# An attention block with a computed bias and two MLPs: key and value loads placed between the first bias rows, three bias rows of VectorE placed one softmax later

## The chip, the cores and the metric

The kernel runs on one core of a Trainium2 chip. The metric is the device time of one execution in microseconds (us); several runs give a median, and one further execution was recorded by the hardware profiler.

## What is computed

The reference, cut to what matters here (B, H, S, D = 2, 8, 576, 64):

```python
scores = scale * np.matmul(q, k.transpose(0, 1, 3, 2))
pos = np.arange(S)
rel = (pos[:, None] - pos[None, :]).astype(np.float32)
psi_rel = np.log1p(np.abs(rel))
psi_i = np.log1p(np.maximum(pos[:, None].astype(np.float32), 1.0))
x = (psi_rel / psi_i)[..., None]
h = np.maximum(x @ w1 + b1, 0.0)          # hidden 32
bias = h @ w2                             # one value per head
scores = scores + bias.transpose(2, 0, 1)[None, :, :, :]
attn = softmax(scores)                    # written out with max, exp, sum
out = np.matmul(attn, v)
x = out.transpose(0, 2, 1, 3).reshape(B * S, H * D)
x = gated MLP of RMS-normalized x         # 512 -> 1536 -> 512, weights in float64
return squared-ReLU MLP of x              # 512 -> 2048 -> 512, weights in float64
```

The bias depends on the head and on the two positions alone, so it is computed once for both batches.

## The kernel before, in words

**Bias rows.** The 576 query positions are cut into 36 groups g of 16. For each group `hidden(g)` makes four tiles `hq` (128 partitions: 4 positions by 32 hidden units), each one multiply and max over the key distances (L182 on VectorE, on ScalarE by L178 for some of the early groups, and the fourth tile on GpSimd from group 12 on). `bias_mm(g)` (L202) multiplies them with w2 on TensorE, and `bias_out(g)` (L221 on ScalarE; L219 on VectorE for group 20 alone) takes the result to a tile `br` with one row for each position and head. The first eight groups go straight to their place: the DMA at L229 writes `br` into every eighth partition of the bias tile (`bias[0][g:P:8]`, 16 partitions of 8 heads). Later groups go to DRAM (`rows<-br`, L225) and come back shifted into place (`bias<-rows`, L239), again into every eighth partition.

**Attention.** A unit u is a tile of 128 queries (nine tiles, four head pairs each: 36 units). `scores_mm(u)` (L261) writes two PSUM tiles from a ring of two, so it waits until the softmax of the unit before has read them. `soft(u, e)` on VectorE (L273) adds the bias and takes the maximum, `expo` on ScalarE (L280) takes the exponential, the transposes (L289, L291, L316) turn the result, copies (L298, L318) bring it to SBUF, and `values_mm(u)` (L339) multiplies with the values. Units 0 to 7 use the bias tile of the first 128 positions (groups 0 to 7), units 8 to 15 that of groups 8 to 15, and so on. So `soft(0, 0)` needs all eight direct bias rows, and `soft(8, 0)` needs the rows of groups 8 to 15, which went over DRAM.

**Order.** The order on every engine is written out by hand. A first loop over s from -2 to 7 does one unit in a step; step s holds the bias of one group (`groups(s)`: at s = -2 groups 0 to 7, at s = -1 groups 8 to 10, then group s + 11), the scores and softmax of unit s + 1, the transposes of unit s, the hidden tiles of group s + 13 and the values of unit s - 1. A second loop from s = 8 (`PAIRED`) on does two units in a step. At its start `finish` steps (L359 to L390) also normalize the attention output of a finished tile and turn it for the MLP: `finish_c` (L386 transposes on TensorE) needs `finish_n` (L380 on VectorE).

**Loads.** All transfers named here are issued by SyncE (the queue SP), in order. Keys and values are loaded head pair by head pair and batch (`load_k(n)`, 288 KB, and `load_v(n)`, 320 KB, n from 0 to 7; units 0 to 7 use n = u, and later units use the same tiles again). `load_k(0)`, `load_k(1)` and `load_v(0)` stand at the start; the others stand at the head of the steps, as the diff shows.

Of the kernel before, what the change touches and what calls it, by code (L numbers as in the profile page):

```python
# [45 lines left out]
PAIRED = 8  # L46
# [6 lines left out]
def tile_kernel(ctx: ExitStack, tc: tile.TileContext, q, k, v, ltab, lg, cst, cst2, rms_g, wg, wv, wo, win, wo2, s_p, b_p, out):  # L53
    nc = tc.nc
# [51 lines left out]
    cb = ac.tile([P, 2], F32, name="cb")  # L106
    spot = ac.tile([P, 1], F32, name="spot")
    owed = []
    g_row = tab_p.tile([1, DM + P], F32, name="g_row")
    mh = const.tile([P, 1], F32, name="mh")  # L110
    g_bc = const.tile([P, DM], F32, name="g_bc")
# [23 lines left out]
    def load_k(n):  # L135
        ks[n] = ac.tile([P, S], F32, name=f"ks{n}")
        nc.sync.dma_start(out=ks[n], in_=k[:, n])

    def load_v(n):
        t = ac.tile([P, 10, D], F32, name=f"vs{n}")  # L140
        nc.sync.dma_start(out=t, in_=v[:, n])
        vs[n] = t
# [23 lines left out]
    def reach(g):  # L166
        return S if g < 8 else max(16 * g + 15, S - 1 - 16 * g) + 1

    def hidden(g, owed):
        hms[g] = []  # L170
        d = reach(g)
        for tq in range(4):
            n = 4 * g + tq
            hq = h_p.tile([P, S], F32, name="hq")[:, :d]
            src = near[:, P - 1 - 4 * n:P - 1 - 4 * n + S] if g < 8 else tab[:, :d]
            hms[g].append(hq)
            if tq == ACT_QUAD and g in ACT_EARLY:
                nc.scalar.activation(hq, src, AF.Relu, bias=nthr[:, n:n + 1], scale=w1_sb)  # L178
                continue

            def go(eng, hq=hq, src=src, n=n):
                eng.tensor_scalar(hq, src, w1_sb, thr[:, n:n + 1], op0=ALU.mult, op1=ALU.max)  # L182

            if tq != POOL_QUAD or g < POOL_FROM:
                go(nc.vector)
            elif owed is None:
                go(nc.gpsimd)
            else:
                owed.append(lambda go=go: go(nc.gpsimd))
# [58 lines left out]
    def chunk(u):  # L248
        tt = TILES[u // 4]
        return tt // 2 if tt < 8 else 4  # L250
# [14 lines left out]
    def soft(u, e, ps):  # L265
        if u % 4 == 0 and e == 0:
            sums[u // 4] = st_p.tile([P, H], F32, name="rs")
        if e == 0:
            prs[u] = pr_p.tile([P, 2 * S], F32, name="pr")
        h = 2 * (u % 4) + e  # L270
        sn = sn_p.tile([P, S], F32, name="sn")
        nm = st_p.tile([P, 1], F32, name="nm")
        nc.vector.tensor_tensor_reduce(out=sn, in0=ps, in1=bias[chunk(u)][:, h, :],  # L273
                                       scale=-1.0 / SCALE, scalar=3.0e38, op0=ALU.add, op1=ALU.min, accum_out=nm)
        sns[u, e] = sn, nm
# [179 lines left out]
    for g in range(AHD, NG):  # L455
        plan[g - 11 if g > 10 else -1].append(g)

    def hide(g, owed=None):
        if g < NG:
            hidden(g, owed)  # L460

    def s_view(i):
        return reg[:, :16 * TJ].rearrange("p (s i c t) -> p s i c t", s=4, i=2, c=2)[:, :, i]
# [34 lines left out]
    for g in range(LEAD):  # L498
        hide(g)
        if g == 0:  # L500
            nc.scalar.activation(cb[:, 0:1], pcb[:, 0:1], AF.Copy, scale=SCALE)
            nc.scalar.activation(cb[:, 1:2], pcb[:, 0:1], AF.Copy, scale=m_sb)
    def groups(s):
        for g in plan[s]:
            pb = bias_mm(g)
            bias_out(g, pb)
            if s == -1 and g == AHD:
                hide(11)
            if s == -2:
                hide(g + LEAD)  # L510

    for s in range(-2, PAIRED):
        r = s % 4
        if s >= 5 and r == 1:
            finish_a(s // 4 - 1)
        if s >= 0 and r == 0:
            load_q(s // 4 + 1)
        if -1 <= s < 5:
            load_k(s + 3)
        if 0 <= s < 7:  # L520
            load_v(s + 1)
        landed = list(rows)[:2 if s > 3 else 1]
        if s != -1:
            groups(s)
        for g in landed:
            bias_in(g)
        if s >= 6 and r == 2:
            finish_b(s // 4 - 1)
        if 0 <= s + 1 < NU:
            ps = scores_mm(s + 1)  # L530
            if s == -1:
                groups(s)
                nc.tensor.matmul(pg, g_row[:, DM:], g_row[:, :DM], start=True, stop=True)
            soft(s + 1, 0, ps[0])
        if 0 <= s < NU:
            turn_out(s, 0, turn_mm(s, 0))
        if s == 7:
            finish_n(0)
        if 0 <= s + 1 < NU:
            expo(s + 1, 0)  # L540
            soft(s + 1, 1, ps[1])
        if 0 <= s < NU:
            for e in (1, 2):
                turn_out(s, e, turn_mm(s, e))
        if 0 <= s + 1 < NU:
            expo(s + 1, 1)
        if s == 0:
            nc.scalar.copy(g_bc, pg)
        if s >= 6 and r == 2:
            finish_s(s // 4 - 1)  # L550
        if s >= -1:
            hide(s + 13)
        if s == 4:
            nc.sync.dma_start(out=s_sb, in_=s_p)
            nc.sync.dma_start(out=b_sb, in_=b_p)
        if 0 <= s - 1 < NU:
            values_mm(s - 1)
        if s >= 5 and r == 1:
            finish_t(s // 4 - 1)
        if s == 6:  # L560
            xs = [act_p.tile([P, NKC, NT], F32R, name=f"xs{i}", tag=f"x{i}") for i in range(2)]
        if s >= 7 and r == 3:
            finish_c(s // 4 - 1)
# [7 lines left out]
    def wait_for(t):  # L571
        nc.gpsimd.tensor_copy(out=spot, in_=t)

    for s in range(PAIRED, NU + 2, 2):
        tile_ends = s % 4 == 0 and s <= NU - 4
        hiding = s + 13 < NG
        if s % 4 == 0:
            load_q(s // 4 + 1)
        for g in list(rows):
            bias_in(g)  # L580
        if s + 1 < NU:
            ps = scores_mm(s + 1)
            for e in range(2):
                soft(s + 1, e, ps[e])
            if s % 4 == 2:
                finish_s(s // 4 - 1)
        for d in range(2):
            if s - 2 + d > PAIRED - 2:
                values_mm(s - 2 + d)
            if s + 1 < NU:  # L590
                expo(s + 1, d)
            if d and tile_ends:
                finish_a(s // 4 - 1)
            if d:
                hide(s + 13, owed)
                hide(s + 14, owed)
            groups(s + d)
        if s in BITS:
            part = bits_of(BITS[s])
        next(part, None)  # L600
        if s % 4 == 0 and (s, 0) in SUMS:
            wait_for(bits_out())
            s_do(*SUMS[s, 0])
        if s % 4 == 2 and not hiding and s < 34:
            finish_n(s // 4 - 1)
            if (s, 0) in SUMS:
                wait_for(fin[s // 4 - 1][0][:, :1])
                s_do(*SUMS[s, 0])
        if s % 4 == 2 and hiding:
            finish_n(s // 4 - 1)  # L610
        if s + 2 < NU:
            ps = scores_mm(s + 2)
            for e in range(2):
                soft(s + 2, e, ps[e])
                if e == 0 and owed:
                    wait_for(sns[s + 2, 0][1])
                    while owed:
                        owed.pop(0)()
        mid = {}
        if s + 2 < NU:  # L620
            mid = {"e0": lambda: expo(s + 2, 0), "e1": lambda: expo(s + 2, 1)}
        if tile_ends:
            mid["fin"] = lambda: finish_t(s // 4 - 1)
        if s % 4 == 2 and s < 34:
            mid["fin"] = lambda: finish_c(s // 4 - 1)
        if s == 36:
            finish_c(7)
        if s % 8 == 4:
            for g in list(rows)[:1]:
                bias_in(g)  # L630
        turns(s, mid)
        if tile_ends:
            finish_b(s // 4 - 1)
            if (s, 1) in SUMS:
                wait_for(ris[0][:, :1])
                s_do(*SUMS[s, 1])
        if s % 4 == 2:
            next(part, None)
        if s == 34:
            finish_n(s // 4 - 1)  # L640
        if s == 26:
            gen.close()
            wpools["ab"] = ring(ctx, "wab", 2)
            wpools["sp"] = ring(ctx, "wsp", 4)
            u_p = pool(ctx, "u", 1)
            reg_p = pool(ctx, "reg", 1)
            reg = reg_p.tile([P, 6 * NT], F32R, name="reg", tag="reg")
            us = [u_p.tile([P, 2, TJ], F32, name=f"us{i}", tag=f"u{i}") for i in range(4)]
        for at, fn, n in TAIL:
            if at == s:  # L650
                fn(n)
        if s == 34:
            s_do(*SUMS[s, 1])
        if s == 34:
            sco.close()
            psC = ring(ctx, "psC", 4, space=PSUM)
# [455 lines left out]
```

## Time and profile before

| | before |
|---|---|
| median of 3 runs | 596.91 us (596.03 to 598.53) |
| the profiled execution | 597.67 us, span 595.7 us |
| TensorE busy | 587.0 us, 99% |
| VectorE busy | 441.7 us, 74% |
| ScalarE busy | 337.8 us, 57% |
| GpSimd busy | 239.1 us, 40% |

The span is the time from the first to the last instruction in the profile; the profiled execution's own time lies 2.0 us above it. PE is TensorE's matmuls, PEld its weight loads, DVE is VectorE, ACT ScalarE, POOL GpSimd, SP SyncE. Busy is the share of time in which an instruction runs; a busy engine need not be the one that others wait for. In a row of the trace, what stands in brackets at the end is the engine's idle time before the instruction and what ended it.

### The profile page before, as it was taken

To read this page: it belongs to the slowest core of one execution; us is meant where nothing else is said; L and a number is where in the kernel's file an instruction comes from. 1 tells how busy PE (TensorE), PEld (TensorE's weight loads), DVE (VectorE), ACT (ScalarE), POOL (GpSimd) and SP (SyncE) were. 2 spreads that over 40 slices of the span, in tenths; PEclk is the share of its full clock that TensorE was granted. 3 is DMA by queue.
4 is the path that set the end of the run, shared out by engine and by line. 5 is a ranking of instruction groups with operands and counts; after the bars stand their busy time and mean duration, and the time that the engine had idled before them with its cause. 6 is when DMAs were issued, how large, how long until landed. Compare 5 with 4: busy or idle time off the path is not lost.

```text
span 595.7 us, 13412 instructions
## 1 busy us (share of the span) xinstructions
PE 587.0 (99%) x5366; PEld 529.9 (89%) x5366; DVE 441.7 (74%) x789; ACT 337.8 (57%) x678; POOL 239.1 (40%) x222
## 2 busy tenths in 40 slices
PE   9999899999999999999999999999999999999997
PEld 5466666667789999999999999999999999999996
DVE  7977989977776887788787944559995336999541
ACT  8887688887775555555656432246662235665110
POOL 0522255450566655655644432323333233333320
PEclk9999999999999999999999999999999999999999
DMA  7898446475012232233223222212222322222321
GB/s 207 260 301 247 154 141 180 142 233 136 24 53 72 72 111 102 72 104 109 72 73 106 84 95 106 89 54 95 83 72 106 107 72 70 72 100 78 127 87 53
DMA packets 25743, 67.26 MB, mean 113 GB/s; under 512 B 3121, under 2 KB 4689, under 8 KB 25682
## 3 DMA queue, kind: packets, MB, share of 16 engines
q1 hardware_dynamic: 25634, 66.40, 34.7%
q8 instruction: 42, 0.69, 0.5%
q14 instruction: 19, 0.16, 0.1%
q10 hardware_dynamic: 48, 0.02, 0.0%
HBM read 53.21 MB, written 10.83 MB: 108 GB/s over the span
## 4 chain that ended last, share of the span: by engine, by line
PE 86%; DMA 5%; DVE 3%; ACT 3%; POOL 1%; issue 1%; SPq 0%; DVEq 0%; ACTq 0%; POOLq 0%
PE c L736 11%; PE c L712 8%; PE c L713 8%; PE c L711 8%; PE b L736 7%; PE po L339 6%; PE b L712 6%; PE b L713 6%; PE b L711 6%; PE a L261 5%; PE b L289 4%; DMA vs<-in_v 3%; PE b L202 3%; PE po L712 2%; PE po L713 2%; PE po L711 2%
## 5 line engine op out<-in xcount | busy, mean ns | idle before, releaser
L447 POOL TENSOR_TENSOR wlo<-wa,whi 128x512 fp32r<-128x512 f32 (+1 forms) x71 | 95.7, 1351 | 75.1 <-ACT whi L444 75.1
L421 POOL TENSOR_SCALAR wa<-wa 128x512 f32<-128x512 f32 x68 | 47.6, 700 | 125.4 <-ACT wa L420 123.1
L273 DVE CUSTOM_DVE_ANT_0 sn<-a,bias 128x576 f32<-128x576 f32 x72 | 51.6, 753 | 16.5 <-PE a L261 8.2
L280 ACT ACTIVATE pr<-sn,nm 128x576 f32<-128x576 f32 x72 | 56.6, 788 | 12.4 <-DVE nm L273 12.4
L420 ACT ACTIVATE wa<-wraw 128x512 f32<-128x512 f32 x68 | 45.9, 676 | 31.1 <-DMA wraw<-in_wo 28.0
L444 ACT CAST whi<-wa 128x512 fp32r<-128x512 f32 x68 | 42.0, 617 | 23.1 <-DVE wa L432 22.9
L182 POOL TENSOR_SCALAR hq<-tab,c_sb,thr 128x384 f32<-128x384 f32 (+17 forms) x24 | 43.5, 1819 | 28.7 <-PE b L202 28.7
L429 DVE TENSOR_SCALAR wa<-wa 128x512 int32<-128x512 int32 x46 | 28.8, 625 | 31.5 <-POOL wa L421 31.5
L712 PE MATMUL c<-f,whi 128*128 128x384 f32 (+1 forms) x150 | 49.7, 331 | 0.0
L713 PE MATMUL c<-f,wlo 128*128 128x384 f32 (+1 forms) x150 | 49.7, 331 | 0.0
L711 PE MATMUL c<-f,whi 128*128 128x384 f32 (+1 forms) x150 | 49.7, 331 | 0.0
L736 PE MATMUL c<-xs,whi 128*128 128x384 f32 x184 | 46.8, 335 | 0.0
L261 PE MATMUL a<-ks,q 64*64 64x352 f32 (+1 forms) x576 | 44.6, 415 | 0.2 <-ACT br L221 0.2
L969 DVE SCALAR_TENSOR_TENSOR f<-hv,b_sb,f 128x384 fp32r<-128x384 f32 x48 | 40.8, 854 | 1.9 <-ACT f L968 1.8
L339 PE MATMUL po<-pt,vs 128*32 128x128 f32 (+1 forms) x1344 | 41.0, 264 | 0.0
L339 PEld LDWEIGHTS po<-pt,vs 128*32 128x32 f32 x1344 | 33.2, 110 | 8.8 <-issue 8.3
L965 DVE SCALAR_TENSOR_TENSOR hv<-sg,s_sb 128x384 f32<-128x384 f32 x48 | 36.4, 758 | 5.9 <-ACT sg L964 5.9
L289 PE MATMUL b<-ident,pr 128*128 128x128 f32 x288 | 39.3, 279 | 1.1 <-DVE br L219 1.1
L261 PEld LDWEIGHTS a<-ks,q 64*64 64x64 f32 x576 | 19.3, 132 | 23.1 <-issue 5.3
L792 POOL TENSOR_TENSOR tl<-ut,th 128x512 fp32r<-128x512 f32 x20 | 25.9, 1296 | 33.4 <-ACT th L791 21.8
L289 PEld LDWEIGHTS b<-ident,pr 128*128 128x128 f32 x288 | 30.8, 141 | 9.3 <-issue 7.7
L736 PE MATMUL b<-xs,whi 128*128 128x384 f32 x152 | 38.7, 335 | 0.0
(201 smaller groups left out, 1649.4 us busy)
## 6 DMA issues: line engine op xcount, KB each, us to landing
wraw<-in_wo SPq DMA_DIRECT2D x28, 512.0 KB, 3.5
bias<-rows SPq DMA_DIRECT2D x32, 288.0 KB, 4.6
rows<-br SPq DMA_DIRECT2D x28, 295.5 KB, 3.1
wraw<-in_win SPq DMA_DIRECT2D x16, 512.0 KB, 3.5
wraw<-in_wg SPq DMA_DIRECT2D x12, 512.0 KB, 3.5
wraw<-in_wv SPq DMA_DIRECT2D x12, 512.0 KB, 3.9
vs<-in_v SPq DMA_DIRECT2D x8, 320.0 KB, 6.6
ks<-in_k SPq DMA_DIRECT2D x8, 288.0 KB, 6.7
```

The costliest lines, as they stand in the source:

```text
L261: nc.tensor.matmul(ps[e][qc, f], qt[u // 4][ed, hp, qc], ks[b[i % len(b)] * NP + hp][ed, f], start=True, stop=True, tile_position=(e * D, ...
L273: nc.vector.tensor_tensor_reduce(out=sn, in0=ps, in1=bias[chunk(u)][:, h, :], scale=-1.0 / SCALE, scalar=3.0e38, op0=ALU.add, op1=ALU.min, ...
L280: nc.scalar.activation(prs[u][:, e * S:(e + 1) * S], sn, AF.Exp, bias=nm, scale=-1.0, accum_out=sums[u // 4][:, h:h + 1])
L289: nc.tensor.transpose(pT[:, c * P:(c + 1) * P], pr[:, o:o + P], ident)
L339: nc.tensor.matmul(dst, w, a, start=c == 0, stop=c == NQC - 1, tile_position=(0, o))
L420: nc.scalar.activation(a.bitcast(F32), raw[:, :, 1].bitcast(F32), AF.Abs)
L421: nc.gpsimd.tensor_scalar(a.bitcast(F32), a.bitcast(F32), F64_MAX, F64_MIN, op0=ALU.min, op1=ALU.max)
L447: nc.gpsimd.tensor_tensor(out=lo[:, c:c + step], in0=w[:, c:c + step].bitcast(F32), in1=hi[:, c:c + step].bitcast(F32), op=ALU.subtract)
L711: nc.tensor.matmul(ps, hi[:, ws], ah, start=first, stop=False)
L712: nc.tensor.matmul(ps, hi[:, ws], al, start=False, stop=False)
L713: nc.tensor.matmul(ps, lo[:, ws], ah, start=False, stop=last)
L736: nc.tensor.matmul(ps, w[i][:, (c0 + c) * P:(c0 + c + 1) * P], a[h][c], start=first and c == 0 and i == 0 and h == 0, stop=c == 1 and i == ...
```

## The change

Loads of keys 2 to 4 and values 1 to 3 are issued between the direct bias rows of groups 0 to 5, one behind each. The seven others follow one in a step from s = -1 to s = 5 (two loads in a step stood at s = 0 to 4 before, and one each at s = -1, 5 and 6). In the first step of the pairs, s = 8, the three VectorE instructions of group 22 (`hide(s + 14)`) are kept back and issued behind `soft(11, 1)`, in the next step of two.

```diff
@@ -106,6 +106,7 @@
+    kept = []
@@ -166,7 +167,7 @@
-    def hidden(g, owed):
+    def hidden(g, owed, kept=None):
@@ -182,7 +183,7 @@
             if tq != POOL_QUAD or g < POOL_FROM:
-                go(nc.vector)
+                go(nc.vector) if kept is None else kept.append(lambda go=go: go(nc.vector))
@@ -500,6 +501,10 @@
+    EARLY = [[x] for x in ((load_k, 2), (load_v, 1), (load_k, 3), (load_v, 2), (load_k, 4), (load_v, 3))] + [[], []]
+    LOADS = {-1: [(load_k, 5)], 0: [(load_v, 4)], 1: [(load_k, 6)], 2: [(load_v, 5)], 3: [(load_k, 7)],
+             4: [(load_v, 6)], 5: [(load_v, 7)]}
@@ -508,6 +513,8 @@
             if s == -2:
                 hide(g + LEAD)
+                for fn, n in EARLY[g]:
+                    fn(n)
@@ -515,10 +522,8 @@
-        if -1 <= s < 5:
-            load_k(s + 3)
-        if 0 <= s < 7:
-            load_v(s + 1)
+        for fn, n in LOADS.get(s, ()):
+            fn(n)
@@ -582,6 +587,8 @@
             for e in range(2):
                 soft(s + 1, e, ps[e])
+            while kept:
+                kept.pop(0)()
             if s % 4 == 2:
                 finish_s(s // 4 - 1)
@@ -593,7 +600,7 @@
                 hide(s + 13, owed)
-                hide(s + 14, owed)
+                hide(s + 14, owed, kept if s == PAIRED else None)
```

The order of SyncE's queue at the first bias rows, before (the number behind `ks` or `vs` is the program's buffer, not n):

```order
L141 DMA vs_139<-in_v 128x640
L229 DMA bias<-br 16x8x576 x8
L137 DMA ks_348<-in_k 128x576
L225 DMA rows_368<-br 128x591
L225 DMA rows_386<-br 128x591
```

and in the changed kernel, from the same load of values on, up to the sixth bias row:

```order
L142 DMA vs_139<-in_v 128x640
L230 DMA bias<-br 16x8x576
L138 DMA ks_208<-in_k 128x576
L230 DMA bias<-br 16x8x576
L142 DMA vs_230<-in_v 128x640
L230 DMA bias<-br 16x8x576
L138 DMA ks_252<-in_k 128x576
L230 DMA bias<-br 16x8x576
L142 DMA vs_274<-in_v 128x640
L230 DMA bias<-br 16x8x576
L138 DMA ks_296<-in_k 128x576
L230 DMA bias<-br 16x8x576
```

Six loads now stand ahead of the last two bias rows, where none stood before; no other engine's order changes here.

VectorE's order at the passage to pairs, before (the rows of 352 elements are group 21, those of 368 group 22, and the softmax behind them is that of unit 10):

```order
L182 TENSOR_SCALAR hq<-tab,c_sb,thr 128x352 x3
L182 TENSOR_SCALAR hq<-tab,c_sb,thr 128x368 x3
L219 TENSOR_SCALAR br<-b,c_sb,cb 128x256
L219 TENSOR_SCALAR br<-b,c_sb,cb 128x335
L273 ISA sn,nm<-a,bias 128x576
```

and in the changed kernel:

```order
L183 TENSOR_SCALAR hq<-tab,c_sb,thr 128x352 x3
L220 TENSOR_SCALAR br<-b,c_sb,cb 128x256
L220 TENSOR_SCALAR br<-b,c_sb,cb 128x335
L274 ISA sn,nm<-a,bias 128x576
L274 ISA nm 128x1
```

Group 22's three instructions no longer stand ahead of `bias_out(20)` and of unit 10's softmax. They come back on VectorE behind the softmax of unit 11 (both its halves) and ahead of the sum of squares of `finish_s`:

```order
L274 ISA sn,nm<-a,bias 128x576
L274 ISA nm 128x1
L274 ISA sn,nm<-a,bias 128x576
L274 ISA nm 128x1
L183 TENSOR_SCALAR hq<-tab,c_sb,thr 128x368 x3
L372 ISA oT,ss<-x 128x512
```

Nothing else moves on VectorE, and the order on TensorE, ScalarE and GpSimd is the same as before.

## Rows read from the trace of the kernel before

**Rows 1.** The page, part 1: busy us (share of the span) and instructions.

```profile
PE 587.0 (99%) x5366; PEld 529.9 (89%) x5366; DVE 441.7 (74%) x789; ACT 337.8 (57%) x678; POOL 239.1 (40%) x222
```

**Rows 2.** Busy time of each engine in three stretches, all instructions.

```profile
core 0: us, PE busy (x) PEld busy (x) DVE busy (x) ACT busy (x) POOL busy (x), PEclk, DMA share, GB/s
...
22.00:56.00 34.00, 33.71 (x542) 21.28 (x546) 26.02 (x69) 29.23 (x70) 14.92 (x10) 1.00 0.99 293
56.00:58.00 2.00, 0.63 (x22) 0.39 (x11) 1.73 (x4) 0.93 (x3) 0.16 (x1) 1.00 0.74 229
...
64.00:68.00 4.00, 2.50 (x22) 1.75 (x24) 3.96 (x11) 2.59 (x7) 1.99 (x3) 1.00 0.52 176
```

**Rows 3.** Timeline of TensorE at the passage: start us, us, what, idle before.

```profile
52.91 1.20 PE L261 MATMUL a<-ks,q 64*64 64x352 f32 x16
...
57.85 0.63 PE L386 MATMUL b<-ident,x 128*128 128x128 f32 x4 [1.37 <-DVE x L380]
...
65.42 0.63 PE L289 MATMUL b<-ident,pr 128*128 128x128 f32 x4 [1.14 <-DVE br L219]
...
67.28 0.44 PE L316 MATMUL b<-ident,pr 128*128 128x128 f32 x2 [0.36 <-DVE pt L298]
...
71.58 0.80 PE L202 MATMUL b<-hq,c_sb 128*32 128x368 f32 x8
...
74.83 0.66 PE L386 MATMUL b<-ident,x 128*128 128x128 f32 x4
```

**Rows 4.** Timeline of VectorE at the passage.

```profile
56.27 0.76 DVE L273 CUSTOM_DVE_ANT_0 sn<-a,bias 128x576 f32<-128x576 f32 x1 [2.89 <-DMA rows<-br]
...
61.94 2.34 DVE L182 TENSOR_SCALAR hq<-tab,c_sb,thr 128x352 f32<-128x352 f32 x6
...
70.36 0.69 DVE L371 CUSTOM_DVE_ANT_0 oT<-x 128x512 f32<-128x512 f32 x1
...
73.34 0.74 DVE L380 SCALAR_TENSOR_TENSOR x<-x,rstd,g_bc 128x512 f32<-128x512 f32 x1
74.00 0.75 DVE L273 CUSTOM_DVE_ANT_0 sn<-a,bias 128x576 f32<-128x576 f32 x1
```

**Rows 5.** Timeline of SyncE's queue: issues of transfers.

```profile
8.26 10.72 SPq L229 DMA_DIRECT2D bias<-br  x8
...
41.71 0.33 SPq L225 DMA_DIRECT2D rows<-br  x1
...
48.13 0.33 SPq L225 DMA_DIRECT2D rows<-br  x1
49.23 1.31 SPq L239 DMA_DIRECT2D bias<-rows  x2
```

**Rows 6.** Transfers issued at 41.7, 50.0 and 18.4 us: KB, us to landing.

```profile
rows<-br SPq DMA_DIRECT2D x1, 295.5 KB, 8.3
...
bias<-rows SPq DMA_DIRECT2D x1, 288.0 KB, 5.9
...
bias<-br SPq DMA_DIRECT2D x1, 288.0 KB, 4.1
```

**Rows 7.** Stretches again: the last two numbers are the DMA share and GB/s.

```profile
9.50:18.50 9.00, 8.76 (x98) 4.07 (x90) 9.00 (x20) 7.88 (x12) 0.00 (x0) 1.00 0.75 204
...
28.00:47.00 19.00, 18.85 (x337) 12.65 (x333) 14.47 (x39) 16.48 (x40) 5.87 (x4) 1.00 1.04 313
34.00:35.00 1.00, 1.00 (x32) 0.83 (x33) 1.00 (x5) 1.00 (x2) 0.00 (x0) 1.00 0.99 190
36.00:37.00 1.00, 1.00 (x20) 0.51 (x16) 0.48 (x2) 0.85 (x4) 0.64 (x1) 1.00 1.04 398
```

**Rows 8.** Timeline of VectorE at the first units.

```profile
22.60 0.76 DVE L273 CUSTOM_DVE_ANT_0 sn<-a,bias 128x576 f32<-128x576 f32 x1 [0.17 <-DMA bias<-br]
...
28.87 0.76 DVE L273 CUSTOM_DVE_ANT_0 sn<-a,bias 128x576 f32<-128x576 f32 x1 [0.39 <-PE a L261]
```

More of the change, by code (lines that the diff above doesn't have):

```diff
@@ L456, in tile_kernel, with hide @@
         plan[g - 11 if g > 10 else -1].append(g)
-    def hide(g, owed=None):
+    def hide(g, owed=None, kept=None):
         if g < NG:
-            hidden(g, owed)
+            hidden(g, owed, kept)
     def s_view(i):
```

## The prediction

> **What bounds the kernel now.** I read the page first: TensorE is busy for 587.0 of the span's 595.7 us [rows 1], so a change gains only where TensorE waits, and loses only where it makes TensorE wait. Next I read the stretches, to find those waits in the first 76 us, where all moved instructions lie [rows 2]. From 22 to 56 us TensorE works for 33.71 of 34.00 us: the steps run at its pace, and neither VectorE (26.02) nor ScalarE (29.23) holds them. Then come two holes: 1.37 us between 56 and 58, and 1.50 us between 64 and 68. Together they are 2.87 us, and that is all that the two parts of the change can give back.
>
> The timelines say what each hole waits for. The first ends when the transposes of `finish_c` get x from VectorE [rows 3]. VectorE is late because `soft(8, 0)`, at 56.27, waited 2.89 us for a transfer [rows 4]. The row names `rows<-br`, but this instruction reads the bias tile of groups 8 to 15, so I go to the transfers that write it. The last is the row of group 15, the second of the two `bias<-rows` issued from 49.23 on, hence at about 50.0 [rows 5]; with 5.9 us to landing [rows 6] it lands at 55.9, and I take it for the one waited for. It could not be issued earlier: its own write to DRAM was issued at 41.71 [rows 5] and took 8.3 us [rows 6], until 50.0. Both are slow because the DMA engines are full there: from 28 to 47 us they are busy at a share of 1.04 and move 313 GB/s [rows 7].
>
> The second hole is three short waits of TensorE; the two largest are 1.14 us for `br` of group 20 (L219) and 0.36 us for a copy of VectorE (L298) [rows 3]. On VectorE both stand behind the six hidden tiles of groups 21 and 22, which take 2.34 us [rows 4].
>
> **The change, part by part.** *The loads that leave the steps.* Of the six loads that move ahead, five would be served after 24 us: two of keys (294.9 kB each) and three of values (327.7 kB each), 1573 kB. From 28 to 47 us 313 GB/s for 19 us are 5947 kB; without these loads some 4400 kB are left, 230 GB/s, a share of about 0.8. The queue is then no longer full, and I price a landing at the 4.1 us of a bias row in the stretch with a share of 0.75 [rows 6, 7]. Group 15's write to DRAM is then down long before it is asked for, and its way back is issued directly behind that of group 14: 48.13 plus 0.33 for the write of group 16 and 0.6 to 0.7 for the issue of group 14, about 49.2 [rows 5]; it lands at 53.3. VectorE is free at 56.27 - 2.89 = 53.4, and the scores of unit 8 end at 54.1 (52.91 + 1.20, [rows 3]). So `soft(8, 0)` starts at about 54.2, 2.0 us earlier, now held by TensorE itself. x follows 1.4 us behind, at 55.7, and TensorE comes to `finish_c` only at 57.85 - 1.37 = 56.5: **the first hole closes, 1.37 us**. Its margin on VectorE is 0.65 us. The ends are 0 (the transfer is still late) and 1.37.
>
> *The three instructions that move behind unit 11's softmax.* They are half of 2.34 us, 1.17 us. `br` of group 20 and unit 10's softmax come earlier by 1.17 + 2.0 = 3.2 us, while TensorE, with the first hole closed, comes earlier by 1.37 and could use 1.50 more, 2.87 in all. ScalarE, with 2.59 us busy of 4.00 [rows 2], is not full. So **the second hole closes, 1.50 us**; if the first does not, moving alone gives the smaller of 1.17 and 1.50. What is late next: behind unit 11 VectorE is ahead by 2.0 us only. The sum of squares goes from 70.36 to 68.4, x from 73.34 to 71.3, `soft(12, 0)` from 74.00 to 72.0 [rows 4]; TensorE would want x, ready 0.7 after its start, at 74.83 - 2.87 = 72.0, and it is there. Group 22's tiles are done at 68.5 (70.36 - 3.2, then 1.17 to run, plus what unit 11's scores hold up); its matmuls would start at 71.58 - 2.87 = 68.7 [rows 3]. I take no loss there, and 0.3 us as the bad end.
>
> *The loads that come between the bias rows.* This is the disputed cost. The eight `bias<-br` are issued from 8.26 on within 10.72 us, the last at 18.4 [rows 5], and that one lands 4.1 us later, at 22.5 [rows 6]. `soft(0, 0)` starts at 22.60, after 0.17 us of waiting for it [rows 8]: no time to spare, and all of VectorE, the scores of unit 1 and the exponentials queue behind. As TensorE then works without holes until 56 us, a delay is not won back in the steps, but for some 0.3 of the 0.39 us that `soft(2, 0)` waited for TensorE [rows 8].
>
> How late does group 7's row land, with 1868 kB of loads ahead of it? Lower end: from 8.3 to 22.5 us about a quarter of the engines' time is free (share 0.75, [rows 7]), 3.5 us, and the load of keys that was served there at 20 us is one of the six, 0.7 more; at the 398 GB/s of a microsecond that loads fill [rows 7] six loads take 4.7 us. Nearly all would fit: no delay. Upper end: a bias row goes no faster in a full queue (190 GB/s in a microsecond that it fills) than alone (204), so if loads and bias rows follow each other all 4.7 us come on top [rows 7]. Between them: at the 313 GB/s of a mixed full queue 8 x 294.9 + 1868 = 4227 kB take 13.5 us, where the bias rows alone take 11.6 at 204 GB/s, 1.9 us more. Bias rows are 56% of the bytes here and about a quarter there, so I go above that: **2.5 us, of which 2.2 count.**
>
> SBUF — State Buffer of the Trainium skill (section "Door 1: The DMA port swizzle") says that a transfer's rate goes with how many of 16 ports its partitions reach, 27.2 GB/s each. Every eighth partition reaches eight ports, so by this rule, as an estimate, a bias row runs at 218 GB/s; the 204 and 190 of [rows 7] agree. Loads over all partitions then lengthen the same eight ports' queue: 8 x 1.35 + 4.3 = 15.1 us instead of 11.6, 3.5 us of delay, and a sum of 597.2. That is rival B below, which is argued from rows.
>
> Sum: -1.37 - 1.50 + 2.2 = -0.67 us. The profiled execution took 597.67 us, 0.76 above the median; the sum is a difference, and I set it against the median: 596.91 - 0.67 = **596.2 us**. A measurement of this kernel can tell about 0.5%, 3.0 us, from no change; the forecast is within that.
>
> **The rivals.** *A, the loads are hidden.* A share of 0.75 speaks for it: the engines have time, and while one transfer's last packets land another can run. Delay under 1 us: 594.0 to 594.7, and only the very end of it, with some luck of the measurement, is faster by over 0.5%. Against it: a bias row alone already moves as slowly as one in a full queue.
>
> *B, slower.* The bias rows are limited by where they write, not by the engines' free time, and the loads go through at their cost: `soft(0, 0)` begins 3.5 to 4.7 us later, 22.60 becomes 26 to 27, and the sum is 597.2 to 598.4. It is slower than before from a delay of 3.2 us on (2.87 + 0.3), and by over 0.5% from 6.2 us on, which would take loads at 300 GB/s that all stand in line. For it: 204 against 190 GB/s.
>
> *C, the passage still waits.* If landings stay at 5 to 6 us, group 15's row lands after 54.1 and the first hole stays in part or whole: 597.6 with the delay as forecast. For it: values 7 now stand ahead of this row where they stood behind it. Against it: the share of 0.8.
>
> **How the numbers follow.** Forecast, delay 1 to 3.5 us: 0.48. A: 0.22. B: 0.21. C: 0.09. The range goes from A's to B's end, 594.2 to 598.4. Faster by over 0.5% is a third of A, 0.07; slower by over 0.5% the tail of B and C, 0.05; within, 0.88.
>
> **What would show it.** In the changed kernel's profile: `soft(0, 0)` with a wait of 2 to 3 us for `bias<-br` (A: under 1; B: over 3.5); a DMA share near 1 from 10 to 24 us and about 0.8 behind 30; no wait for a transfer at `soft(8, 0)`; TensorE's idle time at `finish_c` and between `bias_out(20)` and unit 11's scores gone; no wait of the group 22 matmuls for VectorE. The prediction is wrong if the steps between 26 and 54 us change their pace, which I hold to be TensorE's, or if the early wait is far from 2.5 us.

## The result and the profile after

| | before | after |
|---|---|---|
| median of 6 runs | 597.77 us (596.03 to 598.77) | 604.04 us (602.29 to 605.53) |
| ratio, 95% interval | | 1.0105 (1.0082 to 1.0129) |
| the profiled execution | 597.67 us, span 595.7 us | 604.24 us, span 602.3 us |

The change makes the kernel 6.3 us slower, 1.05%, where the forecast was 0.7 us faster. The forecast was 596.2 us in a range from 594.2 to 598.4, set against the earlier median of 596.91 us, with 0.05 for slower by over 0.5%: it was wrong.

The page's first part shows the loss on TensorE: it works 3.6 us longer at the same instructions, and with a span longer by 6.6 us it is idle 3 us longer [rows 1].

```profile
PE 590.6 (98%) x5366; PEld 531.6 (88%) x5366; DVE 442.7 (74%) x789; ACT 338.4 (56%) x678; POOL 238.0 (40%) x222
```

The granted clock in 40 slices of the span, where 9 is full speed, was 9 throughout before; now the third slice, from 30 us on, is not.

```profile
PEclk9979999999999999999999999999999999999999
```

The next lines are stretches of the changed kernel, to be read like [rows 2] and [rows 7]. The first two lines are where the loads now stand between the bias rows; then follow the steps, the half-clock part of them, and the time in which the steps that stood from 28 to 47 us before stand after a delay of some 9 us.

```profile
10.00:20.00 10.00, 8.55 (x94) 4.13 (x86) 10.00 (x22) 6.91 (x10) 0.00 (x0) 1.00 1.02 268
20.00:28.00 8.00, 5.58 (x48) 1.62 (x46) 3.00 (x8) 3.63 (x6) 3.47 (x2) 1.00 1.04 252
...
28.00:47.00 19.00, 16.92 (x204) 10.15 (x204) 13.01 (x34) 14.43 (x34) 6.03 (x5) 0.82 0.71 215
...
30.00:36.00 6.00, 5.92 (x33) 3.13 (x33) 4.44 (x14) 4.57 (x11) 0.00 (x0) 0.51 0.80 250
...
37.00:56.00 19.00, 19.00 (x348) 12.98 (x344) 14.23 (x37) 15.78 (x38) 5.37 (x4) 1.00 0.77 220
```

With the loads among the rows the DMA engines are busy all the time, but move 268 and then 252 GB/s, not the 313 of the full queue in the steps before. The two former holes can't be looked up as stretches of time, since other instructions stand there now; they are looked up by their instructions.

TensorE's order is the same in both kernels, so each instruction's start can be set against its start before. These are the first units before, in TensorE's timeline: start us, us, what, idle before.

```profile
23.75 1.54 PE L261 MATMUL a<-ks,q 64*64 64x352 f32 x16
25.22 1.09 PE L289 MATMUL b<-ident,pr 128*128 128x128 f32 x8
...
26.74 0.85 PE L202 MATMUL b<-hq,c_sb 128*32 128x384 f32 x8
27.52 1.20 PE L261 MATMUL a<-ks,q 64*64 64x352 f32 x16
```

This is TensorE's timeline after.

```profile
25.99 0.88 PE L203 MATMUL b<-hq,c_sb 128*32 128x400 f32 x8
30.08 2.87 PE L262 MATMUL a<-ks,q 64*64 64x352 f32 x16 [3.21 <-DVE nm L274]
32.88 1.97 PE L290 MATMUL b<-ident,pr 128*128 128x128 f32 x8
...
34.99 1.51 PE L203 MATMUL b<-hq,c_sb 128*32 128x384 f32 x8
36.43 1.42 PE L262 MATMUL a<-ks,q 64*64 64x352 f32 x16
37.78 1.09 PE L290 MATMUL b<-ident,pr 128*128 128x128 f32 x8
...
40.76 1.20 PE L262 MATMUL a<-ks,q 64*64 64x352 f32 x16
...
65.16 0.66 PE L387 MATMUL b<-ident,x 128*128 128x128 f32 x4
...
73.03 0.44 PE L317 MATMUL b<-ident,pr 128*128 128x128 f32 x2
...
77.32 1.10 PE L203 MATMUL b<-hq,c_sb 128*32 128x368 f32 x8
...
81.34 0.63 PE L387 MATMUL b<-ident,x 128*128 128x128 f32 x4 [0.33 <-ACT pt L299]
```

The scores of unit 1 (first L262 row) come behind 3.21 us without work, because `soft(0, 0)` had not read its tile. They take 2.87 us, the eight transposes behind them 1.97 and the eight bias matmuls 1.51, where the same took 1.54, 1.09 and 0.85 before. From 37.78 on the pace is the old one. `finish_c` at 65.16 has no wait any more (1.37 before), but its second instance at 81.34 has one of 0.33.

VectorE's timeline after has `soft(0, 0)`, `soft(8, 0)`, the start of group 22's tiles and the second `finish_n`.

```profile
29.26 0.76 DVE L274 CUSTOM_DVE_ANT_0 sn<-a,bias 128x576 f32<-128x576 f32 x1 [3.97 <-DMA rows<-br]
...
62.99 0.76 DVE L274 CUSTOM_DVE_ANT_0 sn<-a,bias 128x576 f32<-128x576 f32 x1 [0.86 <-PE a L262]
...
76.32 1.23 DVE L183 TENSOR_SCALAR hq<-tab,c_sb,thr 128x368 f32<-128x368 f32 x3
...
80.45 0.75 DVE L381 SCALAR_TENSOR_TENSOR x<-x,rstd,g_bc 128x512 f32<-128x512 f32 x1
```

`soft(0, 0)` starts at 29.26 where it started at 22.60 [rows 8]: 6.7 us late. The row names `rows<-br`, which this instruction doesn't read; its tile is written by the direct rows, and the transfer row shows the one that it waits for. The second row is the transfer of group 7's row, issued at 21.5 us: KB, us to landing. It lands at 29.0. The first row of all, ahead of the loads at 8.7 us, took 3.6.

```profile
bias<-br SPq DMA_DIRECT2D x1, 288.0 KB, 3.6
...
bias<-br SPq DMA_DIRECT2D x1, 288.0 KB, 7.5
```

The account, by instructions of TensorE (the starts before are from [rows 3] and, for the scores of units 1 and 2, from the lines above):

| instruction | before | after | late by |
|---|---|---|---|
| scores of unit 1 | 23.75 | 30.08 | 6.33 |
| scores of unit 2 | 27.52 | 36.43 | 8.91 |
| `finish_c`, first | 57.85 | 65.16 | 7.31 |
| L316, now L317, behind `bias_out(20)` | 67.28 | 73.03 | 5.75 |
| `finish_c`, second | 74.83 | 81.34 | 6.51 |
| span | 595.7 | 602.3 | 6.6 |

So the early wait costs 6.3 us, the matmuls at half clock behind it 2.6 more, the first hole gives 1.6 back, the second 1.6, and 0.8 are lost again at the second `finish_c`. Nothing that matters happens behind it.

### The profile page after: what moved, and what is told of

Read it like the earlier page. It is cut to its first block, busy times and chain, and to the rows that moved or that the text cites. A ratio compares the mean times of both kernels' runs of the same rounds, so it can differ in the third digit from the quotient of the medians.

```text
span 602.3 us, 13411 instructions
## 1 busy us (share of the span) xinstructions
PE 590.6 (98%) x5366; PEld 531.6 (88%) x5366; DVE 442.7 (74%) x789; ACT 338.4 (56%) x678; POOL 238.0 (40%) x222
## 4 chain that ended last, share of the span: by engine, by line
PE 89%; DVE 3%; DMA 3%; ACT 2%; issue 1%; POOL 1%; DVEq 0%; ACTq 0%; SPq 0%; POOLq 0%
PE c L743 11%; PE c L719 8%; PE c L718 8%; PE c L720 8%; PE b L743 7%; PE po L340 7%; PE a L262 7%; PE b L719 6%; PE b L720 6%; PE b L718 6%; PE b L290 5%; PE b L203 3%; DMA bias<-br 2%; PE po L719 2%; PE po L718 2%; PE po L720 2%
## 5 line engine op out<-in xcount | busy, mean ns | idle before, releaser
L430 DVE TENSOR_SCALAR wa<-wa 128x512 int32<-128x512 int32 x46 | 28.8, 625 | 32.8 <-POOL wa L422 32.8
L262 PE MATMUL a<-ks,q 64*64 64x352 f32 (+1 forms) x576 | 46.0, 425 | 6.0 <-DVE nm L274 3.2
L262 PEld LDWEIGHTS a<-ks,q 64*64 64x64 f32 x576 | 19.5, 135 | 30.5 <-issue 6.0
L183 DVE TENSOR_SCALAR hq<-tab,c_sb,thr 128x448 f32<-128x448 f32 (+17 forms) x87 | 37.5, 495 | 2.3 <-PE b L203 2.3
```

The lines of the kernel that those rows point to most:

```text
L262: nc.tensor.matmul(ps[e][qc, f], qt[u // 4][ed, hp, qc], ks[b[i % len(b)] * NP + hp][ed, f], start=True, stop=True, tile_position=(e * D, ...
```

## The experiments

The theory that I tested first: the early loads alone make the loss, each by its turn in SyncE's queue, and the half clock is a consequence of TensorE's wait. The rivals: the moved VectorE instructions cost something; the rows wait for their `br` buffers and not for the transfers; the loss is the clock's. All diffs are against the changed kernel, and each ratio is against the kernel before on the same chip.

**The moved instructions alone.** The early loads are taken out.

```diff
-    EARLY = ... (cut)
-    LOADS = ... (cut)
-                for fn, n in EARLY[g]:
-                    fn(n)
-        for fn, n in LOADS.get(s, ()):
-            fn(n)
+        if -1 <= s < 5:
+            load_k(s + 3)
+        if 0 <= s < 7:
+            load_v(s + 1)
```

> The three instructions behind unit 11's softmax alone, loads as before. Theory (the early loads make the whole loss): the wait of 2.9 us at soft(8, 0) stays; TensorE's second hole of 1.5 us shrinks by 1.2 to 1.5, and about 0.7 us come back as a wait of finish_c for x at 75 us: 0.5 to 0.8 us faster than before. Rival (the move of the three instructions costs by itself): 0 to 1 us slower.

Measured: 597.77 us, ratio 0.9995 (0.9982 to 1.0008): no difference that can be told, and the 0.5 to 0.8 us expected lie inside this interval too. TensorE's timeline of this kernel shows why so little is left.

```profile
57.94 0.63 PE L387 MATMUL b<-ident,x 128*128 128x128 f32 x4 [1.19 <-DVE x L381]
...
70.54 1.10 PE L203 MATMUL b<-hq,c_sb 128*32 128x368 f32 x8
...
74.55 0.63 PE L387 MATMUL b<-ident,x 128*128 128x128 f32 x4 [0.32 <-ACT pt L299]
```

The first hole stays (1.19 us). Group 22's matmuls start 1.04 us earlier than before (71.58, [rows 3]), then take 1.10 instead of 0.80, since they wait for tiles that are now made late, and at the second `finish_c` 0.28 us are left of the gain. Moving the three instructions shortens one wait and makes two small new ones.

**The early loads alone.** The three instructions go back to their place.

```diff
-                hide(s + 14, owed, kept if s == PAIRED else None)
+                hide(s + 14, owed)
```

> The early loads alone, the three instructions where they were. Theory: soft(0, 0) at about 29 us, TensorE's clock at half for some 7 us behind it, the wait at soft(8, 0) gone: about 7 us slower than before (8.9 lost, 1.6 to 2 won). Rival (the passage makes part of the loss): under 6 us slower.

Measured: 604.76 us, ratio 1.011 (1.009 to 1.013). The whole loss is here. `soft(0, 0)` starts at 30.69, and this kernel's trace names the transfer itself:

```profile
30.69 0.76 DVE L274 CUSTOM_DVE_ANT_0 sn<-a,bias 128x576 f32<-128x576 f32 x1 [3.11 <-DMA bias<-br]
```

The clock did not fall where it was expected. In this execution it is at half from 19.9 to 26.7 us, ahead of the long wait and behind two waits for ScalarE (1.00 and 1.60 us), and at half once more from 34 to 36 us:

```profile
19.90:26.70 6.80, 6.00 (x32) 1.76 (x36) 1.78 (x5) 2.13 (x4) 0.00 (x0) 0.50 1.05 218
```

The scores of unit 2 start at 36.66, 9.1 us late, about as after (8.9).

**The six loads behind the last direct row.** They still stand ahead of all steps, but no direct bias row stands behind them any more.

```diff
-    EARLY = [[x] for x in ((load_k, 2), (load_v, 1), (load_k, 3), (load_v, 2), (load_k, 4), (load_v, 3))] + [[], []]
+    EARLY = [[]] * 7 + [[(load_k, 2), (load_v, 1), (load_k, 3), (load_v, 2), (load_k, 4), (load_v, 3)]]
```

> The changed kernel with all six early loads behind the eighth bias row instead of between the rows. Theory (only loads ahead of group 7's row in the queue cost): soft(0, 0) at 22.6 us or up to 1 us later, no fall of the clock, both holes at the passage closed: 1.5 to 3 us faster than before. Rival (loads cost wherever they stand near the bias rows, since the rows of groups 8 to 10 and their buffers queue behind them): 0 to 3 us slower.

Measured: 599.15 us, ratio 1.0011 (0.9997 to 1.0025): most of the loss is gone, but the 1.5 to 3 us that the theory expected are not gained. The first row is VectorE's `soft(0, 0)`, the second ScalarE's next wait, the third TensorE's wait for it, in the timelines of this kernel.

```profile
23.50 0.76 DVE L274 CUSTOM_DVE_ANT_0 sn<-a,bias 128x576 f32<-128x576 f32 x1 [0.34 <-DMA bias<-br]
...
31.90 1.09 ACT L222 ACTIVATE br<-b,cb,c_sb 128x384 f32<-128x384 f32 x2 [2.31 <-DMA rows<-br]
...
33.04 0.33 PE L292 MATMUL b<-ident,pr 128*128 128x128 f32 x1 [2.56 <-ACT br L222]
```

The place among the rows makes the early wait: behind them the loads leave 0.34 us of it. `soft(0, 0)` is 0.9 us late here, of which 0.6 stand ahead of all loads, since the first row was issued at 8.87 us instead of 8.26. But the six loads now stand ahead of the rows of the next groups to DRAM. `br` has four buffers, a buffer is free only when its row has left, and so ScalarE waits 2.31 us for one, and TensorE 2.56 us for ScalarE. The loss has moved to the next user of the queue.

**Matmuls in the wait.** In the step s = -1 TensorE gets 14 matmuls more, whose result nothing reads.

```diff
+                keep_clock(7)
```

> The changed kernel with seven idle matmuls of the identity (they compute nothing that is used) on TensorE behind the bias groups 8 to 10, to fill its wait at 27 to 30 us. Theory (the wait lowers the granted clock and this costs 2.5 us beyond the wait itself): granted clock 1.00 from 30 to 37 us, 2 to 2.5 us faster than the changed kernel, so 3.5 to 4.5 us slower than before. Rival (the clock falls for another reason or costs nothing): like the changed kernel, 6 us slower than before.

Measured: 602.59 us, ratio 1.0083 (1.0061 to 1.0105), 1.45 us under the changed kernel's median, where the theory expected 2 to 2.5 and the rival nothing; the intervals of the two ratios overlap. The first two rows are stretches of this kernel, the others are TensorE's timeline, with the added matmuls at L156.

```profile
22.00:26.00 4.00, 4.00 (x28) 1.13 (x24) 0.54 (x2) 0.59 (x2) 0.00 (x0) 0.50 1.07 231
30.00:36.00 6.00, 5.87 (x64) 3.26 (x64) 5.96 (x15) 5.43 (x15) 3.22 (x3) 1.00 0.72 224
...
28.72 1.83 PE L156 MATMUL b<-ident 128*128 128x128 f32 x14
...
34.66 1.20 PE L262 MATMUL a<-ks,q 64*64 64x352 f32 x16
```

From 30 to 36 us the clock is now full, and the scores of unit 2 start at 34.66, 1.8 us earlier than after. But in this execution the clock was at half from 22 to 26 us, behind two other waits of TensorE (1.83 and 1.33 us for ScalarE), and that is ahead of the added matmuls, which start at 28.72. They can't have caused this earlier fall: the early loads alone show it without them. So this run doesn't separate what the added matmuls do from where the clock happened to fall, and it doesn't test the cost of the clock.

**Two loads between the rows, four behind.**

```diff
-    EARLY = [[x] for x in ((load_k, 2), (load_v, 1), (load_k, 3), (load_v, 2), (load_k, 4), (load_v, 3))] + [[], []]
+    EARLY = [[(load_k, 2)], [(load_v, 1)]] + [[]] * 5 + [[(load_k, 3), (load_v, 2), (load_k, 4), (load_v, 3)]]
```

> The changed kernel with two of the six early loads between the bias rows (keys 2 behind group 0's row, values 1 behind group 1's) and the other four behind the eighth row. Theory A (every load ahead of group 7's row costs its own time, about 1.1 us of the 6.7): soft(0, 0) at 24.5 to 25.5 us, 2 to 3 us slower than all six behind the rows. Theory B (two fit into the free quarter of the engines' time, the delay comes only once the queue is full): soft(0, 0) before 23.5 us, within 1 us of all six behind the rows.

Measured: 599.36 us, ratio 1.0026 (1.0015 to 1.0037). By the ratios that is some 0.9 us slower than with all six behind the rows, not 2 to 3. VectorE's hidden tiles and `soft(0, 0)` in this kernel, and ScalarE's wait for the buffers in the list of waits (us in total, times, longest):

```profile
24.17 1.68 DVE L183 TENSOR_SCALAR hq<-tab,c_sb,thr 128x400 f32<-128x400 f32 x4 [3.28 <-PE b L203]
25.77 0.75 DVE L274 CUSTOM_DVE_ANT_0 sn<-a,bias 128x576 f32<-128x576 f32 x1
...
ACT br L222 <- DMA bias<-br: 2.7, 2, 2.3
```

Group 7's row was issued at 20.6 us and landed 4.7 later, at 25.3, which is 2.8 us later than before. The first row was issued 0.65 us later (8.91 instead of 8.26), so the two loads make some 2.2 us of it. After, six loads make 6.5 less 0.45, about 6.0. That is 1.1 and 1.0 us for a load: there is no free time that takes up the first ones. `soft(0, 0)` itself, 3.2 us late, doesn't show this: it did not wait for the row, but stood behind hidden tiles for which VectorE had waited 3.28 us for TensorE. TensorE was at a clock of 0.51 from 21 to 24.5 us, behind a wait of 1.87 us for ScalarE, and ScalarE had waited for the buffers of rows still under way (2.3 us at 18.5). The later wait for a buffer, which cost 2.31 us with six loads behind the rows, is absent with four.

**Eight buffers for `br`.**

```diff
-    br_p = ring(gen, "br", 4)
+    br_p = ring(gen, "br", 8)
```

> The changed kernel with eight buffers for the bias rows instead of four, so that ScalarE need not wait for a row's transfer before it writes the row four groups later. Theory (the transfers are the limit, and they work without a pause from 10 to 28 us): group 7's row lands within 1 us of 29.0 as before, still 5 to 7 us slower than before. Rival (the four buffers hold the last rows back): it lands 2 us earlier or more, 2 to 4 us slower than before.

Measured: 603.81 us, ratio 1.0108 (1.0091 to 1.0126), as the changed kernel. VectorE's timeline and the transfer of group 7's row, issued at 19.4 us:

```profile
29.02 0.76 DVE L274 CUSTOM_DVE_ANT_0 sn<-a,bias 128x576 f32<-128x576 f32 x1 [6.35 <-DMA bias<-br]
...
bias<-br SPq DMA_DIRECT2D x1, 288.0 KB, 9.4
```

The row is issued 2.1 us earlier and lands at 28.8, against 29.0 after. With four buffers ScalarE waited for transfers too (up to 2.45 us at a time), with eight it doesn't up to this point, and the row comes no earlier for it: the transfers are the limit here, and the buffers are not.

This trace also shows the clock's cost a second time. TensorE waits in one piece here, and the clock is at half from about 28.5 to 35 us.

```profile
29.84 2.86 PE L262 MATMUL a<-ks,q 64*64 64x352 f32 x16 [5.83 <-DVE nm L274]
32.63 1.97 PE L290 MATMUL b<-ident,pr 128*128 128x128 f32 x8
...
35.66 1.20 PE L262 MATMUL a<-ks,q 64*64 64x352 f32 x16
```

The scores of unit 1 are 6.1 us late and those of unit 2 8.1: 2.1 us more, where it was 2.6 after.

**The rows written to all partitions.** The same bytes go from the same tile to another place, so the bias that the first units read is not the reference's.

```diff
-            nc.sync.dma_start(out=bias[0][g:P:8, :, :], in_=br[:, :to])
+            nc.sync.dma_start(out=bias[0][:, 7 - g, :], in_=br[:, :to])
```

> The changed kernel with the eight direct bias rows written to all 128 partitions (one head's slice of the bias tile for each group, so the bias that the first units read is not the reference's) instead of every eighth; bytes, packets and order as before. Theory (where the rows are written limits them and, behind them in the queue, the loads): a row and a load no longer add up to more than the 1.48 us of a group, and group 7's row lands at 22 to 24 us instead of 29.0. Rival (the bytes limit): it lands at 27 us or later.

Measured, one execution: 599.66 us. The stretch that was 268 GB/s after, and the transfer of group 7's row, issued at 20.6 us:

```profile
10.00:20.00 10.00, 8.59 (x90) 3.32 (x85) 10.00 (x23) 7.28 (x11) 0.00 (x0) 1.00 0.97 307
...
bias<-br SPq DMA_DIRECT2D x1, 288.0 KB, 4.3
```

The row lands at 24.9, 4.1 us earlier, and the engines move 307 GB/s at no larger share. That is later than the theory's 22 to 24 and earlier than the rival's 27. In this execution 4.1 of the 6.5 us between the landings before (22.5) and after (29.0) go with where the rows are written. The same rows without the loads were not run, so what the loads alone still cost there is open.

**Three loads behind the last direct row**, and the later ones in the steps, where there is one load fewer in each of the steps -1, 3 and 4 than before.

```diff
-    EARLY = [[x] for x in ((load_k, 2), (load_v, 1), (load_k, 3), (load_v, 2), (load_k, 4), (load_v, 3))] + [[], []]
-    LOADS = {-1: [(load_k, 5)], 0: [(load_v, 4)], 1: [(load_k, 6)], 2: [(load_v, 5)], 3: [(load_k, 7)],
-             4: [(load_v, 6)], 5: [(load_v, 7)]}
+    EARLY = [[]] * 7 + [[(load_k, 2), (load_v, 1), (load_k, 3)]]
+    LOADS = {0: [(load_k, 4), (load_v, 2)], 1: [(load_k, 5), (load_v, 3)], 2: [(load_k, 6), (load_v, 4)],
+             3: [(load_k, 7)], 4: [(load_v, 5)], 5: [(load_v, 6)], 6: [(load_v, 7)]}
```

> A version that might beat both: keys 2, values 1 and keys 3 behind the eighth bias row, then two loads a step (keys 4 to 6, values 2 to 4) at s = 0 to 2, and one a step (keys 7, values 5, 6, 7) at s = 3 to 6; group 22's three instructions moved as in the change. Theory: no row of the first eight is delayed, the queue is empty enough when group 15's row needs it, so the first hole closes (1.4 us), the second too (1.2 to 1.5), 0.7 us come back at finish_c: 1.5 to 2.2 us faster than before. Rival (three loads ahead of the rows of groups 8 to 10 already make ScalarE wait for a buffer, as six did for 2.3 us): within 0.7 us of before.

Measured: 596.74 us, ratio 0.9981 (0.9972 to 0.9991). VectorE's `soft(0, 0)` and `soft(8, 0)` in this kernel:

```profile
22.79 0.76 DVE L274 CUSTOM_DVE_ANT_0 sn<-a,bias 128x576 f32<-128x576 f32 x1
...
55.90 0.76 DVE L274 CUSTOM_DVE_ANT_0 sn<-a,bias 128x576 f32<-128x576 f32 x1 [2.53 <-ACT pt L299]
```

The early cost is gone, but `soft(8, 0)` still waits 2.53 us (2.89 before), and 1.01 us of the first hole is left; the queue is full from 28 to 47 us as before (share 1.02). What is gained comes mainly from the second hole: 1.1 us by the ratio, where 1.5 to 2.2 were expected. That the first hole closes only when the loads are really taken out of these steps does not follow, though: in the last two versions below the share there is 1.03 and 1.04, and the first hole is closed.

**Six loads behind the last direct row and eight buffers.** Both edits above together.

> All six early loads behind the eighth bias row, with eight buffers for the bias rows instead of four. Theory (behind the rows the loads cost only by the buffer that group 12 waits for, 2.3 us with four): this wait is gone, both holes at the passage close (1.4 and 1.5 us), 0.7 us come back at finish_c: 1.5 to 2.5 us faster than before. Rival (another wait for the full queue takes the buffer's place, for instance for the keys or values of the first units): within 0.7 us of before.

Measured: 596.30 us, ratio 0.9973 (0.9959 to 0.9988). ScalarE's timeline at the place of the 2.31 us, and TensorE's two `finish_c`:

```profile
29.52 1.15 ACT L222 ACTIVATE br<-b,cb,c_sb 128x384 f32<-128x384 f32 x2
...
57.63 0.63 PE L387 MATMUL b<-ident,x 128*128 128x128 f32 x4 [0.33 <-DVE x L381]
...
74.24 0.63 PE L387 MATMUL b<-ident,x 128*128 128x128 f32 x4 [0.33 <-ACT pt L299]
```

Here the buffers do matter: with the loads behind the rows, they are what let ScalarE run on, and the wait of 2.31 us is gone. The 1.6 us gained lie in the expected 1.5 to 2.5. Eight buffers in the kernel before, without any load moved, were not run.

**The same, with three instructions kept back in every step of two.**

```diff
-                hide(s + 14, owed, kept if s == PAIRED else None)
+                hide(s + 14, owed, kept)
```

> The same, and in every step of two the second group's three VectorE instructions go behind the following softmax, not in the first such step alone. Theory (the 0.7 us at finish_c come from the three moved instructions that stand ahead of x, beside the six of groups 23 and 24): with group 24's three behind the next softmax x comes earlier and the 0.7 us are won, 2.2 to 3 us faster than before. Rival (it only moves the wait one step on, where VectorE has no more room): like the run without it.

Measured: 596.98 us, ratio 0.9979 (0.9968 to 0.9991). At the second `finish_c` TensorE is 2.7 us ahead of before (72.14 against 74.83), but the gain is 1.3 us and not the 2.2 to 3 expected. Further on the matmuls of a kept group wait for their tiles, and the lead is given back at three places of before's timeline: 88, 106 and 124 us. The row is TensorE's first such place in this kernel; before, the same matmuls stood at 88.80 and took 0.91 us.

```profile
86.19 1.53 PE L203 MATMUL b<-hq,c_sb 128*32 128x432 f32 x8
```

**The same, kept back in the first two steps of two only** (`s in (PAIRED, PAIRED + 2)`).

> As all six loads behind the rows with eight buffers, and the second group's three instructions moved behind the next softmax in the first two steps of two (groups 22 and 24). Theory: x at finish_c comes as early as with all of them moved (0.7 us won at 74 us), and the later bias groups, whose tiles stay where they were, do not give 1.6 us back at 88, 106 and 124 us: 2.5 to 3 us faster than before. Rival (the wait only moves on, to group 24's matmuls or to the next finish_c): 1 to 2 us faster, like the two runs before it.

Measured: 596.19 us, ratio 0.9975 (0.9959 to 0.9990). TensorE's second `finish_c` starts at 72.39 without a wait, 2.4 us ahead of before:

```profile
56.48 0.66 PE L387 MATMUL b<-ident,x 128*128 128x128 f32 x4
...
72.39 0.66 PE L387 MATMUL b<-ident,x 128*128 128x128 f32 x4
```

This cannot be told from the version above with one step kept. They are 0.25 and 0.27% faster than before, 1.3 and 1.6 us, less than the bound of 0.5% that the prediction set, and not the 2.5 to 3 us expected. The three versions with eight buffers have the same order up to the first `finish_c`, and their profiled executions leave 0.33, 0 and 0 us of the first hole, so a single trace doesn't settle this hole to 0.3 us.

## Why the prediction was wrong

**The step that failed** is the disputed cost: "2.5 us, of which 2.2 count". `soft(0, 0)` came 6.7 us late, and TensorE 6.3; the upper end of 4.7 was too low as well. Some 0.45 us of it stand ahead of every early load: the first row was issued at 8.71 instead of 8.26 us, and though no kernel here moves anything ahead of it, this lies anywhere from 8.16 to 9.02 in their traces. So 6.2 are left. The early loads alone carry the whole loss (1.011), and six loads placed behind the rows leave 0.34 us of that wait.

All three estimates took their rates from other places. The upper end served loads and rows in turn, the loads at 398 GB/s; the six loads' 1868 kB in 6.2 us are 300. The middle estimate took 313 GB/s from the steps, but the full queue moved 252 to 268 here; at these rates its own sum gives 15.8 to 16.8 us, 4.2 to 5.2 more than 11.6, and the 1 to 2 us left to 6.2 stay without an account. The lower end took a share of 0.75 for a quarter of free time; but from 0.75 to 1.02 the rate rose only from 204 to 268, 64 GB/s, so that quarter was no room for six loads at 398. Much of this goes with where the rows are written: sent to all partitions, in one execution, they let 307 GB/s through at a share of 0.97, and group 7's row lands 4.1 us earlier. That all six loads stand in line and go at 300 GB/s is just what rival B named as the condition for 6.2 us of delay; that tail got 0.05, together with C's.

SBUF — State Buffer of the Trainium skill (section "Door 1: The DMA port swizzle") says that the rate goes with the ports reached. The run with rows to all partitions agrees in direction (268 to 307 GB/s); the delay of 3.5 us worked out from its figures was nearer than mine but still too small.

**The term that was missing** is TensorE's clock, 2.6 us. Between 26.9 and 30.1 us it had nothing to do; from 30.1 to 36 the granted clock is 0.51, that is 1.2 instead of 2.4 GHz. Unit 1's scores took 1.3 us longer than before, the transposes behind them 0.9 and the bias matmuls 0.7; by their starts, the delay grows by 2.6 between the scores of units 1 and 2 (6.33 to 8.91). With eight buffers it grows by 2.1 in the same place. The prediction priced a wait of TensorE at its length; its own sign of being wrong, steps that change their pace, came with it. TensorE: Matmul & The Clock Gate of the Trainium skill (section "Part 1: The HAM clock gate") has these two levels, the lower one for an engine that has been idle; the rows agree.

**What was right.** The holes: 1.37 forecast and 1.6 found, 1.50 and 1.6. `soft(8, 0)` waits for TensorE (0.86) and for no transfer, and from 37 to 56 us, where the steps of 28 to 47 now stand, the share is 0.77 and the rate 220 GB/s, forecast about 0.8 and 230. That the emptier queue is what closes the first hole is not shown by this alone, since it also closes with a full one in the last two versions. **"No loss" behind the passage** was wrong by 0.8 us: group 22's matmuls take 1.10 us instead of 0.80, and x for the second `finish_c`, ready at 81.20 (80.45 and 0.75), reaches TensorE only then; with group 24's three instructions kept back as well, this wait is gone. The bad end there was 0.3. The sum with what was measured is 6.3 + 2.6 - 1.6 - 1.6 + 0.8 = 6.5 us at the second `finish_c`, against 6.6 in the spans.

**What stays open.** What the clock costs is read from two traces only. It is at half for some 3 to 9 us in all six kernels that have loads between the rows, but at different times: from 30 to 36 us after, from 20 to 27 and again from 34 to 36 with the early loads alone, from 21 to 27 with the added matmuls, from 28.5 to 35 with eight buffers, from 21 to 24 with two loads and with the rows to all partitions. In the traces of the others it stays full. The run that filled the wait does not settle what a kernel without the fall would take. The loads on another queue were not tried. Which part of the gain of the best versions lies in the buffers and which in the moved instructions is below what these runs can tell.

## What to carry to other kernels

Before a load is moved ahead in a queue, list what stands behind it up to the first instruction that waits without slack, and price it at the rate of that very mix: a busy share below 1 was no measure of room here, where the transfers were slow for where they write. A wait of TensorE costs more than its length when the clock falls behind it, as behind the 3.2 us here, and wants a term of its own. When a prefetch is wanted anyway, put it behind the urgent transfers, and then look for the buffers that the next transfers hold.

## What the runs showed of the hardware

The same 288 KB from the same tile, between the same loads, took 7.5 us written to every eighth partition and 4.3 us written to all 128, in one execution of each. A full DMA share says little of the rate: it went with 218 GB/s (1.05, early loads alone, 19.9 to 26.7 us) and with 313 (1.04, before, 28 to 47 us).

The mean granted clock of an execution goes with the time that TensorE was at half clock: it is 0.997 in the trace with 3.5 us at half (two loads between the rows), 0.994 with some 6.5 (the changed kernel) and 0.992 with some 9 (the early loads alone). The changed kernel was at 0.994 or below in all six executions, and the version with eight buffers and the loads behind the rows at 0.999 or above in all twelve. With six loads behind the rows and four buffers, the seven executions at 0.996 or 0.997 took 598.91 to 599.68 us, the five at 0.999 or 1.000 took 596.97 to 598.71; the kernel before had 5 executions of 23 at 0.996 or 0.997 in that series. One profiled execution does not show this spread, and what decides it was not tried.
